# A cached decode step of two attention and MLP layers: one more part of K per batch kept on the chip, and layer 2's heads moved

## The chip, the cores and the metric

The kernel runs on one core of one Trainium2 chip. A core has a matrix engine (PE, whose weight loads are listed apart as PEld), a vector engine (DVE), a scalar engine (ACT), a general engine (POOL) and a queue engine (SP), which here issues every DMA. There are 16 DMA engines, an on-chip memory of 128 partitions (SBUF) and eight product banks of 128 x 512 float32 (PSUM), into which PE writes. The engines run side by side, each through its own list of instructions in order, and wait for one another by semaphores.

The metric is device time in microseconds (us), the median over runs.

## The reference

Eight sequences (batches) each decode one token of width 448. `_A_ref` is attention with 16 query heads over 8 cached K/V heads of 4096 x 256 (two query heads share one K/V head); `_B_ref` is a small mixer with an MLP, whose shifts move everything out of a sequence of length one, so that its first half adds nothing. The same caches and weights are used twice, in layer 1 and in layer 2:

```python
q = (x @ wq).reshape(B, Sq, Hq, Dh) ...
scores = jnp.einsum("bhqd,bhkd->bhqk", q, k) * (Dh ** -0.5)
p = _softmax(scores, axis=-1)
o = jnp.einsum("bhqk,bhkd->bhqd", p, v)
...
x = x + _A_ref(_layernorm(x, axis=-1), A_k_cache, A_v_cache, A_wq, A_wo)
x = x + _B_ref(_layernorm(x, axis=-1), B_w1, B_w2, B_w3, B_w4)
x = x + _A_ref(_layernorm(x, axis=-1), A_k_cache, A_v_cache, A_wq, A_wo)
x = x + _B_ref(_layernorm(x, axis=-1), B_w1, B_w2, B_w3, B_w4)
```

K and V are 134 MB each in bfloat16, and each is needed in both layers.

## The kernel before, in words

**Units and parts.** A unit is one K/V head of one batch in one layer, written (layer, batch, head): 128 units, and a few gaps (`None`). A unit has four *parts* of K and four of V, each 128 x 2048 bfloat16, 512 KB. A part of K arrives raw in a slot, is transposed by DVE into a second slot (`transposes`, L549, the instruction at L562), and is multiplied by PE with the expanded queries (`k_part`, L642). Then come the maximum (`max_reduce`, `max_mms`), the exponentials on ACT (`exps`), their turning into columns and their sums (`to_rows`, `sums`), and a few steps later the products with V (`v_part`, L620), whose results are scaled by ACT (`head_out`, L593).

**Slots.** The slab has 31 slots of one part each. K of six heads of a batch (`KEEP = 6`) stays after layer 1 for layer 2; two of these 24 parts are kept in four product banks (`park`: written by DVE at L567, brought back to a slot by ACT at L520), 22 in slots, so nine slots are left for what streams. The heads 0 and 1 (`loose`) are loaded again in layer 2. The other four banks are two for scores (`scb`, used by turns), one for the dense work (`dnb`) and one for head outputs and projections (`pyb`).

**Loads.** The list `loads` is written in advance in the order in which the parts are needed. `pump` (L510) is called wherever the program frees a slot; it issues loads while more than `RESERVE` slots are free, two parts in one DMA of 1 MB where two neighbouring slots are free and the stage allows it. With at least `ENOUGH` = 7 parts under way it rather waits for a neighbour than loads one part, in the stages marked `firm`. SP carries the issues out in order, each waiting for its slot's last reader.

**Order of the units.** `units` is written out by hand. For each batch b: layer 1's heads; then, while the *dense chain* of b runs (output projection, MLP, layer 2's queries: `mid_steps`, L261, one step of which is done at the end of each quarter of a unit), a gap, one or two *lone* units whose inputs are ready, and a gap; then (`fence`) layer 2 of batch b, then layer 1 of batch b + 1. In batches 0 to 3 two lone units stand beside the chain (16 quarters of a unit, the chain's larger products in two bursts, `spread`); in 4 to 7 one (12 quarters). For two units the products with V are put off into the chain (`ahead`, `late_v`): in batch b > 0 the loose heads 0 and 1 of layer 2 of batch b - 1; their probabilities wait in `pt_far`, of which there are `AHEAD` = 2. `plan` gives the step of every other `v_part`, six quarters after its K.

**Sharing of banks.** Head outputs go into `pyb` in turn, four columns each, 112 places, zeroed by a `memset` once (L625). The expanded queries of the next unit are built in columns 448 and up of a score bank (`expand`, L154). The dense work takes four turns of 64 columns in `dnb` (`room`, L203).

Of the kernel before, what the change touches and what calls it, by code (L numbers as in the profile page):

```python
# [21 lines left out]
AHEAD = 2  # L22
# [9 lines left out]
def kernel(  # L32
# [63 lines left out]
    qT2 = consts.tile([128, HJ, 2], BF16, name="qT2")  # L96
# [6 lines left out]
    park = [[ps1.tile([128, 512], FP32, name=f"park{i}{q}") for q in range(2)] for i in range(PARKED)]  # L103
# [50 lines left out]
    def expand(blk, qT, n, bank):  # L154

        rp = bank[:, 448 : 448 + 16 * n].rearrange("p (g d e h) -> p g d e h", d=4, e=2, h=2)
# [17 lines left out]
    n_po = (512 - PO) // 4  # L174
    OT = consts.tile([128, HJ, 2], BF16, name="OT")
# [27 lines left out]
    def room(n):  # L203

        turn[0] = (turn[0] + 1) % 4
        return dnb[:, 64 * turn[0] : 64 * turn[0] + n]
# [54 lines left out]
    def mid_steps(b, spread):  # L261
# [15 lines left out]
        hT = work.tile([128, HC], BF16, tag="hT", bufs=1)  # L277
# [7 lines left out]
        def gelu():  # L285
# [16 lines left out]
                    out=hT[:], in0=hu, scalar=1.0, in1=hx, op0=ALU.add, op1=ALU.mult  # L302
# [32 lines left out]
        q2 = qT2[:, :, b % 2].rearrange("p (i m) -> p i m", i=2)  # L335
# [33 lines left out]
    parked = {(second[-1], 4 - PARKED + i): i for i in range(PARKED)}  # L369
    GAP = None  # L370
    ahead = {b: [(2, b - 1, g) for g in loose] for b in range(1, Bn)}
    ahead[0], ahead[6] = [(1, 1, g) for g in loose], [(2, 5, 0), (1, 7, 0)]
    lone = {b: [(1, b + 2, g) for g in loose] for b in range(4)}
    lone.update({4: [(1, 6, 0)], 5: [(1, 6, 1)], 6: [(1, 7, 1)], 7: [(2, 5, 1)]})
# [4 lines left out]
    half = 4  # L379
    for b in range(Bn):  # L380
        if b:
            units += [(1, b, g) for g in heads[len(loose) :]]
        else:
            units += [(1, b, g) for g in heads[:5]] + ahead[0] + [(1, b, g) for g in heads[5:]]
        ends[len(units) - 1] = b
        at = 4 * len(units)
        ps = [(units.index(u), s) for u in ahead[b] for s in range(4)]
        late_v.update(zip(ps, [at + i for i in (4, 4, 5, 5, 6, 7, 8, 9)]))
        units += [GAP] + lone[b] + [GAP]
        fence[len(units)] = b  # L390
        units += [(2, b, g) for g in second[:half]] + ahead.get(b + 1, []) + [(2, b, g) for g in second[half:]]
    units += [(2, Bn - 1, g) for g in loose]
# [4 lines left out]

    def fresh(u, s):

        return u is not GAP and (u[0] == 1 or u[2] in loose)  # L400
# [61 lines left out]
    for i in range(4 * n_units + 8):  # L462
# [9 lines left out]
        t, q = divmod(i + 2, 4)  # L472
# [73 lines left out]

    todo = list(reversed(parts))

    def transposes(i):  # L549


        while len(parts) - len(todo) < by[i]:
# [395 lines left out]
```

## Time and profile before

| | |
|---|---|
| median of 3 runs | 1114.37 us (1114.31 to 1114.5) |
| the profiled execution | 1115.99 us |
| its span, first to last instruction | 1114.2 us |
| busy: PE, PEld, DVE, ACT, POOL | 687.9, 640.8, 550.7, 306.0, 104.1 us |
| bytes read from memory | 446.77 MB, 401 GB/s over the span |
| issues of loads of K and V | 605: 227 of 1 MB, 378 of 512 KB |
| from issue to landing, median | 13.1 us (V) and 14.0 us (K) for 1 MB; 8.1 and 8.8 us for 512 KB |

A line of the page's fifth part, or of an answer on groups, reads: line of the kernel, engine, operation, output <- input, shape, count | busy time, mean ns of one | idle time of the engine just before them and what ended it. A line of the waits reads: who waited <- for whom: us in total, times, longest. A line of a table by stretches reads: from:to in us, length, busy us of PE, PEld, DVE, ACT and POOL with the number of instructions, the granted clock of PE as a share, the share of the DMA engines' time, and the GB/s moved. In the page's rows of slices the span is cut into 40 equal ones and a digit is tenths.

### The profile page before, as it was taken

The numbers are of one execution on the slowest core, as the hardware profiler recorded it, in microseconds if no ns is written. First come the engines' busy times: TensorE is split into PE (matmuls) and PEld (weight loads), VectorE is DVE, ScalarE is ACT, GpSimd is POOL, SyncE is SP. The second block draws the span as 40 slices with busy tenths as digits, with TensorE's granted clock in tenths as the row PEclk, the third lists the DMA queues.
The fourth block names the chain that finished last, engine by engine and source line by source line (L and its number), as shares of the span: only waits on it lengthen the run. The fifth ranks groups of instructions, "written<-read, shape, count | busy, mean of one in ns | idle before, by whom it ended". The sixth has DMA issues, their size and how long they took to land.

```text
span 1114.2 us, 46349 instructions
## 1 busy us (share of the span) xinstructions
PE 687.9 (62%) x20737; PEld 640.8 (58%) x20737; DVE 550.7 (49%) x1305; ACT 306.0 (27%) x1360; POOL 104.1 (9%) x156
## 2 busy tenths in 40 slices
PE   3345675666756576565756667565756667665766
PEld 2334565565646565565655556565656566555765
DVE  4347554654446445554455535563446535554322
ACT  1112124321233212422243212422143212422242
POOL 0001001110011100110011000110011000100011
DMA  9999999999999999999999999999999999999993
GB/s 367 394 418 425 408 417 422 424 417 395 417 423 424 400 403 419 423 424 391 414 420 424 402 410 404 420 424 415 383 421 424 409 412 404 422 423 400 371 405 128
DMA packets 94503, 449.77 MB, mean 404 GB/s; under 512 B 9936, under 2 KB 15968, under 8 KB 64864
## 3 DMA queue, kind: packets, MB, share of 16 engines
q1 hardware_dynamic: 94304, 446.81, 98.4%
q8 instruction: 162, 2.65, 0.9%
q14 instruction: 37, 0.30, 0.1%
HBM read 446.77 MB, written 0.01 MB: 401 GB/s over the span
## 4 chain that ended last, share of the span: by engine, by line
DMA 39%; PE 15%; issue 6%; ACT 6%; DVE 5%; POOL 0%; SPq 0%; DVEq 0%; ACTq 0%; POOLq 0%
DMA slab<-in_A_v_cache_dram 31%; DMA slab<-in_A_k_cache_dram 9%; PE bank L630 5%; PE bank L653 4%; DVE slab L562 3%; ACT pt L720 2%; PE bank L137 1%; ACT slab L520 1%; ACT pe L689 1%; DVE small L686 1%; PE bank L676 1%; PE bank L712 1%; ACT pt_far L720 1%; PE bank L702 1%; PE bank L313 1%
## 5 line engine op out<-in xcount | busy, mean ns | idle before, releaser
L562 DVE STREAM_TRANSPOSE slab<-slab 128x512 f32<-128x512 f32 x640 | 414.6, 687 | 214.7 <-DMA slab<-in_A_k_cache_dram 167.2
L630 PEld LDWEIGHTS <-slab 128*128 128x128 bf16 x8192 | 273.1, 106 | 286.5 <-DMA slab<-in_A_v_cache_dram 223.0
L630 PE MATMUL bank<-pt,slab 128*128 128x2 bf16 x7168 | 260.5, 166 | 232.7 <-DMA slab<-in_A_v_cache_dram 161.5
L653 PE MATMUL bank<-Qblk,slab 128*128 128x8 bf16 x8192 | 297.2, 168 | 77.4 <-DVE slab L562 39.1
L653 PEld LDWEIGHTS <-slab 128*128 128x128 bf16 x8192 | 267.8, 105 | 88.2 <-DVE slab L562 46.6
L689 ACT ACTIVATE pe<-bank,small 128x32 bf16<-128x32 f32 x256 | 61.3, 295 | 406.7 <-DVE small L686 406.7
L731 POOL TENSOR_TENSOR small<-small 128x2 f32<-128x2 f32 x112 | 78.2, 698 | 773.2 <-DVE small L727 773.2
L720 ACT CAST pt<-bank 32x64 bf16<-32x64 f32 x448 | 90.8, 203 | 106.4 <-PE bank L712 102.5
L686 DVE TENSOR_REDUCE small<-bank 128x2 f32<-128x256 f32 x128 | 54.1, 423 | 103.2 <-PE bank L676 102.9
L727 DVE TENSOR_REDUCE small<-bank 128x2 f32<-128x64 f32 x128 | 27.1, 212 | 118.5 <-ACT pt L720 102.9
L166 ACT CAST Qblk<-bank 32x32 bf16<-32x32 f32 (+1 forms) x272 | 48.2, 177 | 110.7 <-PE bank L160 108.2
L676 PE MATMUL bank<-rows,small 128*128 128x128 bf16 x256 | 48.5, 293 | 11.5 <-DVE small L668 11.5
L668 DVE TENSOR_REDUCE small<-bank 128x2 bf16<-128x64 f32 x128 | 26.4, 206 | 58.5 <-PE bank L653 58.3
L630 PE MATMUL bank<-pt_far,slab 128*128 128x2 bf16 x1024 | 37.0, 166 | 26.1 <-DMA slab<-in_A_v_cache_dram 24.4
L712 PE MATMUL bank<-pe,rows 128*128 128x64 bf16 x512 | 51.3, 241 | 1.9 <-issue 1.9
L712 PEld LDWEIGHTS <-rows 128*128 128x128 bf16 x512 | 33.8, 124 | 28.4 <-issue 28.1
L702 PE MATMUL bank<-pe,small 128*128 128x64 bf16 x128 | 27.3, 213 | 30.7 <-ACT pe L689 29.4
L182 PEld LDWEIGHTS <-wo_sb 128*128 128x128 bf16 x1152 | 35.5, 104 | 8.8 <-issue 7.7
L182 PE MATMUL bank<-OT,wo_sb 128*128 128x1 bf16 x1024 | 33.2, 165 | 5.6 <-ACT OT L599 4.5
L137 PEld LDWEIGHTS <-wq_sb 128*128 128x128 bf16 x864 | 30.6, 106 | 10.3 <-issue 5.9
L520 ACT COPY slab<-park 128x1024 bf16<-128x1024 bf16 x32 | 30.1, 1029 | 9.4 <-DVE slab L562 9.3
L599 ACT ACTIVATE OT<-bank,small 128x2 bf16<-128x2 f32 x122 | 25.4, 261 | 24.1 <-PE bank L630 22.7
(113 smaller groups left out, 386.5 us busy)
## 6 DMA issues: line engine op xcount, KB each, us to landing
slab<-in_A_v_cache_dram SPq DMA_DIRECT2D x130, 1024.0 KB, 13.1
slab<-in_A_v_cache_dram SPq DMA_DIRECT2D x252, 512.0 KB, 8.1
slab<-in_A_k_cache_dram SPq DMA_DIRECT2D x97, 1024.0 KB, 14.0
slab<-in_A_k_cache_dram SPq DMA_DIRECT2D x126, 512.0 KB, 8.8
wo_sb<-in_A_wo_dram SPq DMA_DIRECT2D x4, 896.0 KB, 11.7
wq_sb<-in_A_wq_dram SPq DMA_DIRECT2D x3, 1024.0 KB, 6.8
w_sb<-in_B_w_dram SPq DMA_DIRECT2D x1, 1568.0 KB, 12.5
w_sb<-in_B_w_dram SPq DMA_DIRECT2D x3, 448.0 KB, 16.7
```

The costliest lines, as they stand in the source:

```text
L137: nc.tensor.matmul(pv[:, i, j, :], cols(big[:, c, :], m + i * half), rows[:, c, :], start=(i == 0 and j == 0 and c == 0), stop=True, skip_ ...
L166: nc.scalar.copy(dst, src)
L182: nc.tensor.matmul(y[:, c, :], chunk(wo_sb[:, k, :], c), o[:, k, :], start=False, stop=True, skip_group_check=True,)
L562: nc.vector.transpose(dst[:, q], src[:, q])
L630: nc.tensor.matmul(pos[t][:, k, :], vv[:, c, 128 * k : 128 * k + 128], pts[t][:, 8 * s + c, :], start=(t == 0 and s == 0 and c == 0 and k ...
L653: nc.tensor.matmul(scs[t][:, 2 * s + c, :, :], ktv[:, db, c, :, x], Qblk[run_of[t][0]][:, run_of[t][1], db, x, :, :], start=(db == 0 and x ...
L676: nc.tensor.matmul(mzs[t][:, 128 * h : 128 * h + 128], pm[:, h : h + 1].to_broadcast([128, 128]), ident, start=True, stop=True,)
L686: nc.vector.tensor_reduce(nm, mx, AX.X, ALU.max, negate=True)
L689: nc.scalar.activation(pe[:].rearrange("p c b h -> p h (c b)")[:, h], scs[t].rearrange("p c b h -> p h (c b)")[:, h], ACT.Exp, bias=nm[:, ...
L712: nc.tensor.matmul(pp[:, c], sel, pe[:], start=True, stop=True)
L720: nc.scalar.copy(pts[t][sl].rearrange("p (k c) h -> p k c h", c=4), pp[sl, :, :, pb, :].rearrange("p c k h -> p k c h"),)
L731: nc.gpsimd.tensor_tensor(out=rz_of[t], in0=zs, in1=mone, op=ALU.pow)
```

## The change

1. **One more part kept.** Part 3 of head 1 of every batch but batch 2 (`stays`) is kept as well, in the spare columns of the four shared banks: three of four column groups of each half in columns 128 to 511 of `dnb` and `pyb`, the fourth in columns 384 to 511 of the score banks. It is a transposed copy by DVE in four pieces. The first is written at once; the others after the maximum of a unit that uses the score bank in question (`at_max`, `put_rest`), and the raw slot is freed after the last. ACT brings them back in four pieces, after head outputs (`at_out`) and after exponentials (`at_exp`), three units ahead of use (`far` = 12). So 25 parts a batch are kept instead of 24, and one load less is in the list for seven batches.
2. **Room for it.** Head outputs have 16 places instead of 112, and half of them is zeroed at a time, fifteen times in all; `room` gives turns of 32 columns; `expand` uses columns 64 and up; `hT` lies over `hu`; layer 1's scaled outputs go into `qT1` instead of `OT`; `qT2` has one buffer.
3. **Order.** Layer 2 of batch b (2, 3, 6, 7, 0, 1, 4, 5) is followed by layer 1 of batch b + 1, as before, but only one lone unit stands beside each chain from batch 1 on, so the chain has 12 quarters there; the lone unit is head 0 of layer 1 of a batch ahead, or, in batches 5 and 7, head 0 of layer 2 of the batch before. Head 1 of layer 1 is an ordinary unit. The products with V that are put off into the chain are those of heads 6, 7, 4 and 5 of layer 2 of batch b - 1: four units instead of two, two parts a quarter.

```diff
-AHEAD = 2
+AHEAD = 4
...
-    park = [[ps1.tile([128, 512], FP32, name=f"park{i}{q}") for q in range(2)] for i in range(PARKED)]
+    park = []
+    for i in range(PARKED):
+        park.append([(q, 0, 4, ps1.tile([128, 512], FP32, name=f"park{i}{q}")[:]) for q in range(2)])
+    spare = [(q, 0, 3, x[:, 128:512]) for q, x in enumerate((dnb, pyb))]
+    park.append(spare + [(q, 3, 4, scb[q][:, 384:512]) for q in range(2)])
...
-        rp = bank[:, 448 : 448 + 16 * n].rearrange("p (g d e h) -> p g d e h", d=4, e=2, h=2)
+        rp = bank[:, 64 : 64 + 16 * n].rearrange("p (g d e h) -> p g d e h", d=4, e=2, h=2)
...
-    n_po = (512 - PO) // 4
+    n_po = (128 - PO) // 4
...
-        return dnb[:, 64 * turn[0] : 64 * turn[0] + n]
+        return dnb[:, 32 * turn[0] : 32 * turn[0] + n]
...
+    parked[(1, 3)] = PARKED
...
-    ahead = {b: [(2, b - 1, g) for g in loose] for b in range(1, Bn)}
-    ahead[0], ahead[6] = [(1, 1, g) for g in loose], [(2, 5, 0), (1, 7, 0)]
-    lone = {b: [(1, b + 2, g) for g in loose] for b in range(4)}
-    lone.update({4: [(1, 6, 0)], 5: [(1, 6, 1)], 6: [(1, 7, 1)], 7: [(2, 5, 1)]})
+    lone = {0: [(1, 2, 0), (1, 2, 1)], 1: [(1, 3, 0)], 2: [(1, 4, 0)], 3: [(1, 5, 0)], 4: [(1, 6, 0)], 5: [(2, 4, 0)], 6: [(1, 7, 0)], 7: [(2, 6, 0)]}
+    mix = [(2, 2), (2, 3), (2, 6), (2, 7), (2, 0), (2, 1), (2, 4), (2, 5), (1, 0), (1, 1), (1, 2), (1, 3), (1, 4), (1, 5), (1, 6), (1, 7)]
+    held_heads = [6, 7, 4, 5]
...
+        hs = [(2, b - 1, g) for g in held_heads] if b else [(1, 1, 0)]
+        ps = [(units.index(u), s) for u in hs for s in range(4)]
+        late_v.update(zip(ps, [at + i for i in (4, 4, 5, 5, 6, 6, 7, 7, 8, 8, 9, 9, 10, 10, 11, 11)]))
...
+    def stays(b, g, s):
+
+        return g not in loose or (g == 1 and s == 3 and b != 2)
...
+        for far in (2, 12):
+            t, q = divmod(i + far, 4)
+            if t < n_units and units[t] and units[t][0] == 2 and stays(*units[t][1:], q) and (units[t][2], q) in parked:
+                if (units[t][2] in loose) == (far > 2):
+                    loads.append(("p", t, q))
...
+    at_out, at_exp, at_max = [], ([], []), ([], [])
+
+    def bring(x, pieces, now):
+
+        dst = slots[x].rearrange("p (e q c x) -> p q c e x", e=4, q=2, c=4)
+
+        def move(q, lo, hi, home):
+            src = home.bitcast(BF16).rearrange("p (c e x) -> p c e x", c=4, e=hi - lo)
+            nc.scalar.copy(dst[:, q, :, lo:hi], src)
+
+        for n, p in enumerate(pieces):
+            if now:
+                move(*p)
+            else:
+                (at_out if n < 2 else at_exp[n - 2]).append(lambda p=p: move(*p))
...
+    def put_rest(t):
+
+        if at_max[t % 2]:
+            raw, rest, n = at_max[t % 2].pop(0)
+            if rest[0]:
+                rest[0]()
+                rest[0] = None
+            rest[1 + n]()
+            if not any(r for r, _, _ in at_max[1 - n] if r == raw):
+                let_go(raw)
...
+                if g in loose:
+                    put(*pieces[0])
+                    rest = [lambda p=p: put(*p) for p in pieces[1:]]
+                    for n in range(2):
+                        at_max[n].append((raw, rest, n))
+                    continue
...
-            if nth[t] == n_po // 2:
-                nc.vector.memset(pyb[:, PO : PO + 4 * (len(order) - n_po)], 0.0)
+            if n > n_po // 2 and n % (n_po // 2) == n_po // 4:
+                at = PO + 2 * n_po * (1 - n // (n_po // 2) % 2)
+                nc.vector.memset(pyb[:, at : at + 2 * n_po], 0.0)
...
+        if at_exp[t % 2]:
+            at_exp[t % 2].pop(0)()
...
                     k_part(t, q)
+                    if q == 3 and at_max[t % 2]:
+                        max_reduce(t)
+                        put_rest(t)
+                        maxed.add(t)
```

## The prediction

> **What bounds the kernel now.** I read the page from the top: busy shares, slices, DMA queues, chain.
>
> ```profile
> PE 687.9 (62%) x20737; PEld 640.8 (58%) x20737; DVE 550.7 (49%) x1305; ACT 306.0 (27%) x1360; POOL 104.1 (9%) x156
> ...
> DMA  9999999999999999999999999999999999999993
> GB/s 367 394 418 425 408 417 422 424 417 395 417 423 424 400 403 419 423 424 391 414 420 424 402 410 404 420 424 415 383 421 424 409 412 404 422 423 400 371 405 128
> ...
> q1 hardware_dynamic: 94304, 446.81, 98.4%
> ...
> DMA 39%; PE 15%; issue 6%; ACT 6%; DVE 5%; POOL 0%; SPq 0%; DVEq 0%; ACTq 0%; POOLq 0%
> ```
>
> No compute engine is above 62%, while the 16 DMA engines are busy in every slice but the last. The busy digit hides something: in slices marked 9 the rate moves between 367 and 425 GB/s. So the kernel is bound by how many bytes are loaded and by how well the queue is kept full. The waits say the same: matmuls that multiply V, and transposes of K, wait for landings.
>
> ```profile
> PE bank L630 <- DMA slab<-in_A_v_cache_dram: 186.0, 158, 4.2
> DVE slab L562 <- DMA slab<-in_A_k_cache_dram: 167.2, 77, 8.9
> ...
> PE bank L630 <- ACT qT L599: 34.6, 18, 6.6
> ...
> PE bank L630 <- ACT OT L599: 11.2, 14, 1.0
> ```
>
> Then I cut the span at the stages: the dense chain of a batch (from its first gap to the fence), layer 2 of that batch, layer 1 of the next. Columns: stretch, length, busy times, granted clock, DMA share, GB/s.
>
> ```profile
> 338.00:382.60 44.60, 28.91 (x918) 27.27 (x916) 23.88 (x51) 11.66 (x56) 4.18 (x6) 1.00 1.01 421
> 382.60:419.60 37.00, 25.57 (x767) 24.04 (x765) 14.90 (x49) 8.31 (x40) 3.34 (x5) 1.00 1.01 394
> 419.60:470.80 51.20, 29.12 (x871) 26.95 (x869) 29.03 (x59) 17.49 (x71) 4.88 (x7) 1.00 1.02 421
> ...
> 648.40:678.00 29.60, 20.29 (x600) 19.31 (x601) 10.99 (x40) 6.53 (x32) 2.64 (x4) 1.00 1.02 414
> ...
> 771.30:802.00 30.70, 20.11 (x604) 19.32 (x604) 12.55 (x42) 6.54 (x32) 2.64 (x4) 1.00 1.00 390
> 802.00:849.10 47.10, 29.32 (x902) 27.84 (x900) 24.79 (x54) 18.09 (x75) 4.88 (x7) 1.00 1.02 417
> ...
> 1016.50:1046.80 30.30, 20.11 (x602) 19.09 (x603) 10.84 (x39) 6.54 (x32) 2.63 (x4) 1.00 1.01 399
> 1046.80:1062.60 15.80, 11.20 (x355) 10.68 (x353) 4.49 (x11) 6.22 (x22) 1.40 (x2) 1.00 0.95 342
> 1062.60:1095.80 33.20, 22.55 (x722) 21.54 (x720) 9.12 (x22) 11.33 (x50) 2.91 (x5) 1.00 0.98 407
> 1095.80:1114.20 18.40, 10.38 (x299) 9.60 (x296) 5.35 (x25) 2.60 (x12) 4.58 (x5) 1.00 0.01 3
> ```
>
> A calm stage runs at 421 GB/s; I call that full rate and price every slower stage by length x (1 - rate/421). Dense chains of batches 1 to 7 run at 400, 394, 396, 414, 390, 412 and 399 and lose 1.9, 2.4, 2.2, 0.5, 2.3, 0.6 and 1.6 us: 11.4 us. Layer 2 loses nothing in batches 1 to 3, 2.1 us in 4 to 6 together and 4.1 us in 7 (rows 342 and 407). Layer 1 loses 3.8 us, most of it (405 GB/s, 1.8 us) ahead of batch 4's chain. The last 18.4 us load nothing.
>
> **The change, part by part.**
>
> *Bytes.* The list of loads falls from 320 to 313 parts of K; V stays at 512. A part is 512 KB, 0.524 MB, 1.245 us at 421 GB/s: 7 x 1.245 = 8.7 us less. DMA issues go from 605 to 604; the pairs of parts (1 MB) among them from 227 to 221. Stretches of single parts stream at 414 at best, 0.02 us more a part, and 5 more parts come singly: 0.1 us, left out. This is the one term on the path throughout: with the queue full, a part less is 1.245 us less.
>
> *The work that replaces those loads.* DVE loses 14 transposes at 687 ns (9.6 us) and gains 28 into the product banks with the same columns in all; by L567 (684 ns for 512 columns) also 9.6 us. ACT gains 28 copies: 1,029 ns for 1,024 columns (L520), two such per part, 7 x 2.06 = 14.4 us. Five more expansions of q (68 to 73) add about 0.25 us of PE and 0.7 us of ACT each. POOL's work is unchanged. DVE is half idle and ACT nearly three quarters; behind them PE waits 186 us for V. Cost taken: nothing; the cover is PE's wait for landings, 23 us a batch, and if it were gone ACT's 14.4 us would be the price.
>
> *Holds on the product banks.* The trace shows a V matmul waiting for ACT's read of another head's columns of the same bank (34.6 and 11.2 us), so two engines take turns at a bank. In the changed order some 15 more V matmuls wait for DVE: the piece of K written into that bank (three quarters of 684 ns, behind a maximum of 206 ns: 0.7 us), and the zeroing of the head sums, now fifteen times instead of once (112 ns; PE waited 1.7 us for the one there is).
>
> ```profile
> L625 DVE MEMSET bank<- x1: 112/112/112, 513.7 to 513.7; 128x64 f32 x1
> ...
>   PE bank L630: 1.7, 1
> ```
>
> ACT's copies back add 0.8 us (V bank) and twice 0.26 us (score banks); the two small pieces 0.2 us each. Per batch 0.7 + 0.8 + 0.5 + 0.4 = 2.4, times 7 = 17, and 14 x 1.7 = 24 of zeroing: 41 us of holds. Behind a held PE queue the V slots, their release and so SP's next issue. It costs time only if all loads issued have landed before PE goes on; 7 to 18 parts are issued ahead, 9 us or more. Bounds 0 and 41 us; I take 1, near the lower end, since PE waits 186 us for landings.
>
> *Dense chains.* From batch 1 on each now has 30 parts to consume in 12 steps (29 in two); before it was 30 in 16 steps (batches 0 to 3) and 22 in 12 (4 to 7). Batch 0's has 26 in 16 and is left as it was. In the short chains the queue thins at the end, where PE waits through the dense steps with no V to free slots: by finer stretches the part after the first gap runs at 412, 386, 413 and 390 GB/s, 0.4, 1.8, 0.4 and 1.4 us lost; the first gap 417, 399, 410 and 417, mean 0.2. In the long ones the first gap is worse (365 in batch 3, 1.1 us), with twice as many K parts, each of which needs two slots. The new chain has the short one's four K parts and the long one's load. I take 0.2 for the gap and 0.8 for the rest, between the 0.5 that 28 us at 414 lose and the short chains' mean of 1.0: 7 x 1.0 = 7.0, 4.4 us better than 11.4. Bounds: 0.7 each (6.5 better); batch 2's 2.4 plus 0.1 for the longer stretch (6.1 worse).
>
> *Layer 2.* With V of heads 6, 7, 4 and 5 put off, V is consumed in twos of heads with two units without between. Counting issues and releases in the order of the program, mostly 7 to 9 parts are under way from the end of the third unit to the sixth, where before there were mostly 8 to 12 in batches 1 to 3. I take 0.6 us a batch, between 0 (those batches) and 0.9 (batch 6 before): 3.6 against 2.1 for six batches, 1.5 worse; bounds 2.1 better, 3.2 worse.
>
> *Layer 1.* The three losses before lie where 7 parts are under way with five slots free, waiting for a neighbour to make a pair. In the new order this occurs in three batches again; 2.8 against 3.8, 1.0 better. Bounds 3.8 better, 0.
>
> *The end.* Batch 7's layer 2 loses 4.1 us: SP issues nothing from 1050.5 to 1056.8 us. Now its chain takes eight more V parts and 11 or 12 instead of 9 or 10 are under way there. I take half back, 2.0; bounds 0 and 3.0. The dense tail of 18.4 us is untouched.
>
> Sum: 8.7 - 1.0 + 4.4 - 1.5 + 1.0 + 2.0 = 13.6 us. The profiled execution took 1115.99 us around a span of 1114.2; it would be 1102.4. The median of the runs, 1114.37, is 1.6 lower: **1100.8 us**.
>
> **Rivals.**
>
> *Only the bytes.* Chains, layer 2 and end lose what they lose now: 1114.4 - 8.7 = 1105.7. For it: the start of a chain is slow in every batch, whatever its length. Against: the losses at its end and in batch 7 have a cause that the new order removes.
>
> *Layer 2 thins.* If its stages run at 407 GB/s, as 1062 to 1096 did, 49 us lose 1.6 in six batches, 9.8 instead of 2.1: 1105.7 + 7.7 = 1113.4, no measurable change. For it: the smaller number under way. Against: before, with 8 or 9 under way for a unit in batch 3, the stage still ran at 421.
>
> *The holds show: slower.* PE, held at the product banks, frees V slots late and the queue runs dry each time. All of the 41 us with the bytes alone: 1105.7 + 41 = 1146.7; it decides once 8.7 us, a fifth of the holds or 1.2 us a batch, reach the queue. For it: 45.8 us of such waits are in the trace already. Against: stages with those waits run at 421.
>
> The Trainium skill has a rule on this ("PSUM — Partial Sum Buffer", section on bank collisions): no two engines may be at one bank and quadrant of partitions at once, so software guards by bank, not by address. By that rule every piece of K in these banks is a hold as counted; were the guard by address the holds, and this rival, would vanish and the sum be 1.0 us better. The trace's 34.6 us agree with the guard by bank.
>
> **How the numbers follow.** Chances: the forecast 0.52, only the bytes 0.20, layer 2 thins 0.14, holds 0.14. Off the forecast's terms the chain alone could cost 10.5 us (from 4.4 better to 6.1 worse), layer 2 another 1.7, the end 2.0: taken as independent, 11 us upward, 1112. Downward 2.1, 3.6, 2.8, 1.0 and 1.0: 5.2, 1095.5. This range leaves out the holds and the upper part of the thin layer 2. A change below 0.2% (2.2 us) can't be told from none here: faster takes the first two cases and two thirds of the third, 0.81; same 0.05; slower 0.14.
>
> **What would show it.** DMA bytes on the queue down by 3.67 MB; dense chains near 38 us at 405 GB/s or more, without the thin stretch before the fence; layer 2 at 415 or more; the stretch after the last fence well above 342. Wrong if chains stay at 395 (only the bytes), if layer 2 falls to about 407, or if waits of the V matmul for DVE and ACT grow by tens of us while the slices show rates below those of before at the same places.

## The result, and the profile after

The changed kernel takes 1110.66 us (median of five, 1108.65 to 1112.04) against 1114.43 for the kernel before on the same chip: a ratio of 0.9961, interval 0.9950 to 0.9972. By the medians that is 3.8 us less, by the ratio, which the rest of the text goes by, 4.3; 13.6 were forecast. The profiled execution took 1112.03 us around a span of 1110.2.

The page of the changed kernel: busy shares, busy tenths and rates of the 40 slices, the load queue, and the engines' shares of the chain that ended last.

```profile
PE 689.6 (62%) x20757; PEld 646.7 (58%) x20757; DVE 552.1 (50%) x1333; ACT 322.3 (29%) x1408; POOL 104.4 (9%) x156
...
DMA  9999999999999999999999999999999999999992
GB/s 360 396 416 423 409 405 419 425 397 416 419 417 405 416 417 425 423 408 397 419 367 424 408 416 409 415 413 407 416 424 425 408 399 390 415 389 414 408 418 92
...
q1 hardware_dynamic: 94160, 443.14, 98.2%
...
DMA 52%; PE 19%; ACT 10%; DVE 10%; issue 7%; SPq 2%; POOL 0%; DVEq 0%; ACTq 0%
```

The bytes fell by the 3.67 MB of seven parts (446.81 to 443.14 MB), yet the rate over the span fell from 401 to 399 GB/s. There are fewer slices at 383 to 395, but a new hole: 367 GB/s in the 21st slice, inside layer 2 of batch 3. In the chain that ended last ACT and DVE stand at 10% each, before at 6 and 5; but the chain of before could be followed back to 318 us only, and its shares add up to 71%. From 318 us on, ACT and DVE are 8 and 7% of it before, 12 and 9% after.

The waits of the changed kernel (who waited <- for whom: us in total, times, longest):

```profile
PE bank L688 <- DMA slab<-in_A_v_cache_dram: 152.9, 154, 3.2
DVE slab L605 <- DMA slab<-in_A_k_cache_dram: 148.6, 55, 10.0
...
PE bank L688 <- DVE bank L683: 19.9, 15, 2.6
PE bank L688 <- ACT qT L650: 15.5, 25, 1.0
...
PE bank L734 <- DVE bank L611: 6.7, 5, 1.9
PE bank L688 <- DVE bank L611: 5.9, 3, 4.3
PE bank L688 <- ACT slab L531: 3.7, 3, 1.2
PE bank L762 <- ACT slab L531: 3.2, 6, 0.9
PE bank L141 <- ACT slab L531: 2.4, 2, 1.2
```

The new holds at the shared banks are there at the size counted. The third line is the zeroing; the last five are the pieces, first DVE's, then ACT's copies back. They are 41.8 us in all, where I counted 41 (19.9 for the 24 of zeroing, 21.9 for the 17 of pieces). The old holds for ACT's read of head outputs fell, from 45.8 to 15.5 us, which I had not counted and which no run explains. With the 1.7 us of the one zeroing before, all holds of this kind rose by 10 us only, from 47.5 to 57.3.

The same cut by stretches (from:to, length, busy us of PE, PEld, DVE, ACT, POOL, granted clock, DMA share, GB/s): chain of batch 2, layer 2, layer 1; chain of batch 3, layer 2, layer 1; layer 2 of batch 6; then the chain of batch 7, its layer 2 in two stretches, and the tail.

```profile
361.70:398.10 36.40, 24.65 (x731) 23.09 (x730) 9.07 (x38) 7.40 (x36) 2.65 (x4) 1.00 1.03 417
398.10:444.40 46.30, 28.85 (x869) 26.87 (x867) 30.81 (x65) 17.61 (x71) 4.90 (x7) 1.00 1.02 422
444.40:493.40 49.00, 31.18 (x963) 28.93 (x960) 29.45 (x62) 13.25 (x64) 4.90 (x7) 1.00 1.01 420
493.40:530.90 37.50, 24.33 (x729) 23.01 (x729) 8.90 (x37) 7.39 (x36) 2.65 (x4) 1.00 1.01 396
530.90:579.60 48.70, 28.59 (x868) 26.79 (x866) 30.71 (x64) 19.26 (x75) 4.90 (x7) 1.00 0.98 390
579.60:627.00 47.40, 30.95 (x964) 29.23 (x963) 28.15 (x59) 13.25 (x64) 4.90 (x7) 1.00 1.01 417
...
920.60:958.90 38.30, 24.60 (x735) 23.06 (x733) 24.73 (x54) 16.94 (x66) 4.20 (x6) 1.00 1.00 393
...
1005.40:1042.00 36.60, 23.16 (x731) 22.49 (x729) 8.89 (x37) 7.40 (x36) 2.64 (x4) 1.00 1.03 410
1042.00:1057.80 15.80, 11.07 (x358) 10.67 (x356) 5.70 (x13) 4.35 (x20) 1.41 (x2) 1.00 1.03 417
1057.80:1090.60 32.80, 21.67 (x689) 20.68 (x687) 9.08 (x23) 15.17 (x56) 3.39 (x5) 1.00 0.94 390
1090.60:1110.20 19.60, 11.22 (x326) 10.44 (x325) 5.35 (x25) 2.61 (x12) 4.11 (x5) 1.00 0.01 3
```

The clock is 1.00 throughout. The chains now run at 396 to 417 over some 37 us, and the stretch behind the last fence rose from 342 to 417, as forecast. Layer 2 does not hold its rate: 390 GB/s in batch 3 and 393 in batch 6, where only batch 7 had lost much before. The tail without loads grew from 18.4 to 19.6 us.

I priced every stretch of a trace as the prediction did, by the bytes of the load queue alone (419 GB/s where the whole moves 421). The us lost, in one profiled execution each, also for five experiments told of below:

| | chains 1 to 7 | layer 2, batches 0 to 6 | layer 2, batch 7 | layer 1 | tail |
|---|---|---|---|---|---|
| before | 11.9 | 3.2 | 4.2 | 3.6 | 18.4 |
| changed | 8.0 | 9.7 | 2.6 | 5.4 | 19.6 |
| no third part | 9.2 | 3.1 | 2.6 | 5.2 | 17.4 |
| third part for nothing | 9.0 | 5.1 | 2.2 | 2.7 | 19.1 |
| less waiting for pairs | 12.2 | 8.5 | 2.2 | 2.5 | 19.0 |
| two heads held (mended) | 13.0 | 8.3 | 5.1 | 0.8 | 19.5 |
| two, in batch 7 four | 13.2 | 9.3 | 2.2 | 2.0 | 19.8 |

From the first row to the second: bytes 8.7 less (3.67 MB at 419 GB/s), chains 3.9 less, the end 1.6 less; layer 2 of the other batches 6.5 more, layer 1 1.8 more, the tail 1.2 more, chain 0 and the first 75 us 0.4 more each. Sum 3.9 less, where the spans differ by 4.0. (Each figure is of one execution, and up to half a us hangs on where the stretches are cut; the same stretch moves by a us between kernels that load in the same order.)

### The profile page after: what moved, and what is told of

The parts are those of the page before. It is cut to its first block, busy times and chain, and to the rows that moved or that the text cites. A ratio compares the mean times of both kernels' runs of the same rounds, so it can differ in the third digit from the quotient of the medians.

```text
span 1110.2 us, 46432 instructions
## 1 busy us (share of the span) xinstructions
PE 689.6 (62%) x20757; PEld 646.7 (58%) x20757; DVE 552.1 (50%) x1333; ACT 322.3 (29%) x1408; POOL 104.4 (9%) x156
## 3 DMA queue, kind: packets, MB, share of 16 engines
q1 hardware_dynamic: 94160, 443.14, 98.2%
## 4 chain that ended last, share of the span: by engine, by line
DMA 52%; PE 19%; ACT 10%; DVE 10%; issue 7%; SPq 2%; POOL 0%; DVEq 0%; ACTq 0%
DMA slab<-in_A_v_cache_dram 39%; DMA slab<-in_A_k_cache_dram 12%; PE bank L688 7%; DVE slab L605 6%; PE bank L711 5%; ACT pt L780 3%; ACT slab L531 2%; ACT pe L747 2%; DVE small L744 2%; PE bank L734 2%; PE bank L772 1%; PE bank L141 1%; SPq L562 1%; ACT pt_far L780 1%; PE bank L762 1%
## 5 line engine op out<-in xcount | busy, mean ns | idle before, releaser
L605 DVE STREAM_TRANSPOSE slab<-slab 128x512 f32<-128x512 f32 x626 | 405.1, 686 | 182.7 <-DMA slab<-in_A_k_cache_dram 148.6
L688 PE MATMUL bank<-pt,slab 128*128 128x2 bf16 x6336 | 230.4, 166 | 187.5 <-DMA slab<-in_A_v_cache_dram 117.1
L791 POOL TENSOR_TENSOR small<-small 128x2 f32<-128x2 f32 x99 | 69.3, 700 | 707.2 <-DVE small L787 707.2
L780 ACT CAST pt<-bank 32x64 bf16<-32x64 f32 x396 | 80.5, 203 | 79.2 <-PE bank L772 75.7
L688 PE MATMUL bank<-pt_far,slab 128*128 128x2 bf16 x1856 | 65.1, 166 | 43.0 <-DMA slab<-in_A_v_cache_dram 35.8
L170 ACT CAST Qblk<-bank 32x32 bf16<-32x32 f32 (+1 forms) x292 | 51.4, 176 | 102.1 <-PE bank L164 99.4
L772 PEld LDWEIGHTS <-rows 128*128 128x128 bf16 x512 | 33.7, 124 | 47.5 <-issue 47.1
L650 ACT ACTIVATE qT<-bank,small 128x2 bf16<-128x2 f32 x198 | 41.8, 266 | 46.8 <-PE bank L688 37.0
L185 PE MATMUL bank<-qT,wo_sb 128*128 128x1 bf16 (+1 forms) x1152 | 38.8, 165 | 8.3 <-ACT qT L650 5.4
L650 ACT ACTIVATE qT<-bank,rz_far 128x2 bf16<-128x2 f32 x58 | 12.2, 265 | 84.6 <-PE bank L688 84.5
L734 PEld LDWEIGHTS <-small 128*128 128x128 bf16 x256 | 17.4, 106 | 31.6 <-DVE small L726 28.4
```

The source lines that it names most:

```text
L170: nc.scalar.copy(dst, src)
L185: nc.tensor.matmul(y[:, c, :], chunk(wo_sb[:, k, :], c), o[:, k, :], start=False, stop=True, skip_group_check=True,)
L605: nc.vector.transpose(dst[:, q], src[:, q])
L650: nc.scalar.mul(qT1[:, k : k + 2, b], pos[t][:, :, h], rz_of[t][:, h : h + 1])
L688: nc.tensor.matmul(pos[t][:, k, :], vv[:, c, 128 * k : 128 * k + 128], pts[t][:, 8 * s + c, :], start=(n_v[0] == 1 and s == 0 and c == 0 a ...
L734: nc.tensor.matmul(mzs[t][:, 128 * h : 128 * h + 128], pm[:, h : h + 1].to_broadcast([128, 128]), ident, start=True, stop=True,)
```

## The experiments

Each kernel was timed against the kernel before on the same chip. The median of before lies between 1114.4 and 1116.7 us on these chips, so I compare ratios; one per mille is 1.1 us. Differences of two ratios are uncertain by about 1.7 per mille, 1.9 us. The ratio of the changed kernel was measured on one chip; that it holds on the chips of the experiments is assumed.

At first there were three theories. **Q**: the load queue runs thin because the planner leaves slots free while it waits for a neighbour, and because the third part takes slots. **H**: PE waits at the shared product banks, and this reaches the queue. **O**: the new order by itself thins layer 2.

**Less waiting for pairs.** `ENOUGH = 7` becomes `ENOUGH = 10`.

> The changed kernel, with ENOUGH raised from 7 to 10: a load of one part waits for a neighbouring slot only while 10 parts or more are under way (660 issues instead of 604, the same bytes). Three theories on why 8.7 us of loads less gave 4: (Q) the queue of loads is thin in layers 1 and 2, because the planner leaves five to nine free slots empty, waiting for a neighbour with seven parts under way, and the third kept part takes slots; (H) the waits at the shared product banks, some 42 us in the trace after, reach the end; (O) the new order of the heads by itself thins layer 2. Q expects 1105 to 1108 us against 1110.7, and the stretches of 264 to 385 GB/s in layer 2 of batch 3 and layer 1 ahead of batches 1, 2 and 7 gone. H and O expect 1110 to 1112, or more for the single parts.

Measured: 0.9961 (0.9943 to 0.9980), the ratio of the changed kernel, so not what Q expects of the planner. Layer 1 loses 2.9 us less and the chains 4.2 more (table). With this order the planner's waiting decides where the queue is thin, not how much is lost.

**Each zeroing 16 times over.**

```diff
-                nc.vector.memset(pyb[:, at : at + 2 * n_po], 0.0)
+                for _ in range(16):
+                    nc.vector.memset(pyb[:, at : at + 2 * n_po], 0.0)
```

> The changed kernel, with each of the 15 zeroings of the head sums done 16 times over: 15 x 85 ns = 1.3 us more each, so the 19.9 us that V matmuls wait for them become some 39. Q and O expect no change that matters, 1109 to 1113 us, since PE then waits that much less for landings. H expects 5 to 19 us more, 1116 to 1130.

Measured: 1.0135 (1.0115 to 1.0154), 19.4 us above the changed kernel by the ratios, 19.6 by the medians. Its waits:

```profile
DVE slab L605 <- DMA slab<-in_A_k_cache_dram: 136.7, 48, 9.1
...
PE bank L689 <- DMA slab<-in_A_v_cache_dram: 121.2, 122, 4.0
...
PE bank L689 <- DVE bank L684: 57.7, 15, 4.7
```

So holds of the V bank do reach the end once they are long enough: 37.8 us more of them (57.7 against 19.9) go with 19.4 us more time. PE's wait for V did shrink, from 152.9 to 121.2 us, as a cover should, and the time rose all the same. SP's waits show the way: a load is issued when its slot's last reader is done, and SP waited 31.7 us longer for V matmuls to be done with slots (first in the changed kernel, then here):

```profile
SPq L562 <- PE bank L688: 258.9, 230, 6.9
```

```profile
SPq L562 <- PE bank L689: 290.6, 217, 6.9
```

But DVE itself was also taken up longer. It is busy 19.1 us more (571.2 against 552.1), and its memsets of 85 ns follow one another with 82 ns between, so that a row of sixteen lasts 2.6 us (from the timeline: start, length), some 37 us more in all. Hence the next one.

```profile
160.17 2.58 DVE L684 MEMSET bank<- 128x32 f32 x16
```

**The same DVE time at no bank.** 23 memsets of two columns in SBUF behind each zeroing.

> The changed kernel with 23 more memsets of two columns in SBUF behind each of the 15 zeroings, about 20 us of DVE time in all, as much as the kernel with each zeroing done 16 times (1130.2 us) but at no product bank. If the 19.6 us there were holds of the bank: 1110 to 1112. If they were DVE's time (K's transposes late): 1128 to 1131.

Measured: 1.0006 (0.9997 to 1.0015), 5.0 us above the changed kernel: neither of the two. The group of the added memsets, in its answer on groups:

```profile
L685 DVE MEMSET small<- 128x2 f32 x345 | 20.7, 60 | 25.7 <-POOL small L793 4.2
```

A row of 23 lasts some 2.8 us here (60 ns each, 67 between), so DVE was taken up for 42 us, a little longer than by the rows of sixteen. The V matmuls wait no longer than in the changed kernel: 19.1 us for 15, going on 0.05 to 0.15 us after the zeroing. So 42 us of DVE's time, 20.7 of them busy, that PE's bank never sees cost 5.0 us, an eighth. The rest of the 19.4, some 14 us, is the hold of the bank. The first half of this was a surprise: DVE is idle half of the time.

**No third part.** `stays` returns `g not in loose`; the seven parts are loaded again.

> The changed kernel without the third kept part: order, banks and zeroing as changed, but part 3 of head 1 is loaded again in layer 2 (8.7 us of loads more, 7 raw slots not held, 7 slots not taken three units ahead, 28 pieces less each way). If the part is worth its bytes (O, or H for the zeroing alone): 1118 to 1120 us. If it pays back part of them in a thinner queue (Q) or in bank waits of its pieces (H): 1112 to 1116, with layer 1 and 2 nearer 419 GB/s.

Measured: 0.9995 (0.9984 to 1.0006). The new order with its zeroing is worth 0.5 us, no more than none, and the third part 3.4 per mille, 3.8 us, of its 8.7, as Q and H expect. Layer 2 loses 3.1 us here (table), no more than before, which speaks against O.

**No third part, and head outputs over 112 places with one zeroing, as before.** On top of the last: `n_po = (512 - PO) // 4`, one `memset`.

> The same without the third part, and with 112 places for head sums and one zeroing as before the change (the 19.9 us of waits for zeroing go). H expects 3 us or more faster than the run without the third part alone; Q and O expect the same time within 1.5 us.

Measured: 0.9986 (0.9976 to 0.9996). The 14 further zeroings cost 0.9 per mille, 1.0 us, if anything, though PE waits 15.0 us for them in the run above. At this size the zeroing's holds are no answer.

**The third part for nothing.** It is neither loaded nor kept: layer 2 multiplies its neighbour in its stead, so the scores of seven parts are those of other columns.

```diff
+        if p == 2 and g in loose and stays(b, g, s):
+            key = u, 2
```

> The changed kernel with the same 313 parts of K loaded, but the third part of a batch is neither put into the product banks nor copied back: layer 2 multiplies the part next to it in its stead (so seven parts of its scores are those of other columns), and the part's slot of layer 1 is let go at once. The kernel without the third part took 1114.0 us, the changed one 1110.7, seven parts at full rate are 8.7 us. If keeping the part costs something (its slots, or its pieces at the shared banks), this gives the rest of the 8.7 us back: 1105 to 1106.5. If bytes not loaded are worth less than full rate in this order, because the queue is thin just there (a part without its neighbour is loaded singly), it stays at 1110 to 1111.

Measured: 0.9922 (0.9910 to 0.9935). Against no third part that is 7.3 per mille, 8.1 us for seven parts: bytes not loaded are worth about their full rate. (The 14 transposes of these parts are left out with them, 9.3 us of DVE in the traces of the two runs, so the 8.1 are not of the bytes alone.) Against the changed kernel it is 3.9 per mille: *keeping* the third part costs 4.3 us.

**The third part written and brought back at once**, so that its slots are held a shorter time: no list `at_max`, `far` 4 instead of 12, four copies in one go.

> The changed kernel, with all four pieces written in one go, so that the raw slot is let go at once (before, after the last piece, up to two units later), and brought back by four copies in one go one unit ahead instead of piece by piece three units ahead. The same pieces, the same banks, the same bytes; a slot held for some 5 and some 8 steps less per batch. If slots are what keeping costs: 1106 to 1108.5, and the stretch after the fence of batch 3 (373 GB/s in the changed kernel) streams at 410 or more. If the waits at the shared banks are what it costs, no gain or a small loss: 1110 to 1113, since DVE and ACT now hold the score banks in longer runs.

Measured: 0.9976 (0.9967 to 0.9985), 1.7 us slower than the changed kernel, if anything. Slots let go sooner don't help; but PE's waits for the pieces are longer here (36.3 us against 21.9), so this run alone doesn't part slots from holds. The next one does.

**The slots of the third part, without its work.** Every step stays in its place, but DVE writes no piece and ACT copies none back (layer 2 multiplies what lies in the slot).

```diff
-                    nc.vector.transpose(dst, src[:, q, :, lo:hi])
+                    if g not in loose:
+                        nc.vector.transpose(dst, src[:, q, :, lo:hi])
...
-            nc.scalar.copy(dst[:, q, :, lo:hi], src)
+            if now:
+                nc.scalar.copy(dst[:, q, :, lo:hi], src)
```

> The changed kernel with every step of the third part in the order of the program (the raw slot held until where its last piece would be written, a slot taken three units ahead of layer 2's head, the maximum taken early) but without its work: no piece is written into the product banks by DVE and none copied back by ACT, so layer 2 multiplies what lies in the slot. The same loads in the same order, the same number of parts under way as the changed kernel at each step. Against the kernel in which the third part costs nothing (7.8 per mille under before) the changed kernel (3.9 per mille under before) loses 4.3 us. If the slots cost them: about 4 per mille under before. If the pieces at the shared banks do: about 7.5 per mille under before. In between: the share of each.

Measured: 0.9922 (0.9910 to 0.9935), the ratio of the kernel in which the part is for nothing. So the slots cost nothing that can be measured, and the theory that I liked best by then fell: Q's second half. The reading that had led me to it was the thin stretch in layer 2 of batch 3. Of the two kernels, one has it and the other not (layer 2's later part, first without the slots, then with them):

```profile
546.00:577.70 31.70, 17.89 (x533) 16.71 (x531) 18.46 (x39) 13.44 (x52) 3.49 (x5) 1.00 1.01 424
```

```profile
546.80:577.60 30.80, 17.75 (x532) 16.62 (x530) 18.58 (x39) 13.53 (x52) 3.49 (x5) 1.00 0.99 391
```

The rate differs by 8%, the length not: the first kernel moved more bytes there and was thin elsewhere. A stage that streams slowly is not by itself lost time.

**Only ACT's copies left out.** The second half of that diff alone.

> The same with DVE's 28 pieces written into the banks, and only ACT's 28 copies back left out (layer 2 multiplies what lies in the slot). Against the one before, it gives the share of DVE's pieces; against the changed kernel, that of ACT's copies (14.4 us of ACT, put at nothing in the forecast). By the priced holds, DVE's pieces (0.7 + 0.4 of 2.4 us a batch) and ACT's copies (1.3 of 2.4) would each be half of what the pieces cost in all.

Measured: 0.9942 (0.9929 to 0.9956). DVE's pieces cost 2.0 per mille, 2.2 us, ACT's copies 1.9 per mille, 2.1 us: about half each, together the 4.3, but each uncertain by 1.9.

**The pieces at other banks.** The same instructions, but the third part lies in the four banks of the two parts parked before, where PE multiplies nothing (the part parked there later overwrites it, so layer 2 multiplies other columns).

```diff
-    spare = [(q, 0, 3, x[:, 128:512]) for q, x in enumerate((dnb, pyb))]
-    park.append(spare + [(q, 3, 4, scb[q][:, 384:512]) for q in range(2)])
+    spare = [(q, 0, 3, park[0][q][3][:, 0:384]) for q in range(2)]
+    park.append(spare + [(q, 3, 4, park[1][q][3][:, 0:128]) for q in range(2)])
```

> The changed kernel, but DVE writes the 28 pieces of the third part into the four banks that hold the two parts parked before, and ACT copies them back from there: the same instructions with the same columns and the same steps, at no bank that PE multiplies into (what the pieces hold is lost to the head parked there later, so layer 2 multiplies other columns at the third part). Against the kernel without pieces (7.8 per mille under before) the pieces cost 3.9 per mille, 4.3 us. If that is the hold of the shared banks: 7.5 to 8 per mille under before. If it is the time of DVE and ACT: 3.5 to 4.5 per mille under before.

Measured: 0.9951 (0.9939 to 0.9964). 1.0 per mille better than the changed kernel, 2.9 worse than without the pieces: 4.9 per mille under before, between the two cases expected. So some 3 of the 4.3 us stay when no bank of PE is touched, which speaks for the work of DVE and ACT rather than the hold. It is not settled: the two shares are not cleanly apart (1.1 and 3.2 us, each uncertain by 1.9), and this kernel has a wait of its own, 6.2 us:

```profile
DVE park L611 <- ACT slab L531: 6.2, 3, 3.4
```

**Two heads held instead of four.** `held_heads = [4, 5]`.

> The changed kernel with V of two heads (4 and 5) instead of four put off into the dense chains from batch 1 on; V of heads 6 and 7 is consumed right behind its scores. 8 parts fewer for each of seven chains (22 for 12 steps). If putting off four heads is what thins layer 2 (7.7 us lost behind the third unit, against 1.2 before): that falls to 4 or less, the chains lose 2 to 4 more, and the time is 1107 to 1111. If the four heads earn what I forecast (4.4 us in the chains, 2.0 at the end) and layer 2 is thin for another reason: 1113 to 1117.

Measured: 1.0027 (1.0016 to 1.0038). This run is spoilt at its end. In `put_rest`, `any(r for r, _, _ in ...)` takes slot number 0 for none, so with batch 7's third part in slot 0 that slot was released twice, and could be given out while in use. In the changed kernel the third part never lies in slot 0. Mended to `any(r == raw ...)`:

> The kernel with V of two heads held, but with every slot released once. In the run before it, slot 0 was released twice in batch 7's stretch: a comparison in the third part's release treats slot number 0 as none, which the changed kernel never meets, and then two loads went to one slot one after the other. If its loss at the end (7.9 us in the last 37 us of loads) was of that, it goes back to the changed kernel's 2 to 3 and the time is 5 us lower: 1112 to 1114. If the two heads themselves thin the end: 1116 to 1118 again.

Measured: 1.0002 (0.9992 to 1.0013), between the two cases expected: the double release had cost 2.8 us. Four heads are worth 4.1 per mille, 4.6 us, over two. Where that comes from shows in the stretches: chain of batch 3 with the three units behind it and the rest of layer 2 in the changed kernel (its layer 1 stands above, from 579.60 on); then the same two and layer 1 in the mended run, and its batch 7 behind the fence:

```profile
493.40:547.20 53.80, 35.18 (x1065) 33.11 (x1065) 19.42 (x58) 12.32 (x57) 4.05 (x6) 1.00 1.01 402
547.20:579.60 32.40, 17.74 (x532) 16.70 (x530) 20.19 (x43) 14.33 (x54) 3.49 (x5) 1.00 0.95 377
```

```profile
503.90:548.50 44.60, 30.82 (x937) 29.24 (x936) 19.54 (x57) 11.46 (x53) 4.04 (x6) 1.00 1.01 393
548.50:586.90 38.40, 21.22 (x661) 19.87 (x658) 19.98 (x43) 14.95 (x58) 3.49 (x5) 1.00 1.01 424
586.90:635.00 48.10, 30.80 (x959) 29.02 (x959) 28.38 (x61) 13.21 (x64) 4.88 (x7) 1.00 1.01 423
1043.20:1059.30 16.10, 10.91 (x356) 10.54 (x354) 4.39 (x11) 6.24 (x22) 1.40 (x2) 1.00 1.01 397
1059.30:1091.80 32.50, 22.01 (x697) 21.02 (x695) 8.85 (x22) 12.86 (x53) 2.79 (x4) 1.00 0.90 368
```

With two heads held, layer 2's later part and layer 1 are at full rate (424 and 423) in nearly every batch, and the chains starve (393, with the units behind them). With four the chains are fuller (402) and layer 2 and layer 1 thin (377 and 417). The loss moves with the V that is moved.

**Two heads, and four in batch 7 alone** (slots released once).

> V of two heads (4 and 5) held in batches 1 to 6 and of four in batch 7, slots released once. In batches 0 to 6 the run with two heads lost 0.5 us in layer 2's later part and layer 1 and about 17 in chains and the units behind them; three heads 8 and 13. By those sums two and three are within 4 us of each other; if the end (2 us with four, 7.9 with two) is what made two heads slow, this is 1107 to 1111.

Measured: 0.9976 (0.9967 to 0.9985), 1112.6 us, just above the range expected if the end is what counts. Of the 4.6 us, 2.9 come from batch 7 and 1.7 from the six batches ahead of it, each uncertain by some 1.6.

**Three heads held: 7, 4 and 5; 3, 4 and 5; 6, 4 and 5** in batches 1 to 6, four in batch 7. The list, for the first:

```diff
-        hs = [(2, b - 1, g) for g in held_heads] if b else [(1, 1, 0)]
+        hs = [(2, b - 1, g) for g in (held_heads if b == Bn - 1 else [7, 4, 5])] if b else [(1, 1, 0)]
```

> The changed kernel with V of three heads (7, 4 and 5) put off into the chains of batches 1 to 6, and of four into that of batch 7; V of head 6 is consumed right behind its scores. With two held, layer 2's later part and layer 1 lost 0.5 us between them in batches 0 to 6 and the chains with the units behind them 17 (with four: 11 and 10). If losses go straight with the number held, three is worth what four is, 1110 to 1112, and only the end is safe. If layer 2 is thin because two heads in a row, 6 and 7, free no V slots, while the chains only need enough V to fill twelve steps, three takes most of both: 1105 to 1108.5, with layer 2's later part at 415 or more in the batches 1 to 6.

> The same with heads 3, 4 and 5 put off, so that V of heads 6 and 7 is consumed ahead of the two heads that load K. In the order of the program 8 or 9 parts more often are under way here at heads 3 and 6, and 11 to 13 at heads 7, 0 and 1. If it is the number held alone that counts: the same as with 7, 4 and 5, within 1.5 us. If it counts where the gap without V lies: up to 3 us slower, with the loss in the first units of layer 2.

> The kernel with V of heads 3, 4 and 5 held, with every slot released once. In the run before it slot 0 was released twice in batch 5 and PE then waited 10 us three times for a load just issued. If that was all of its loss: within 1.5 us of the kernel with heads 7, 4 and 5 (6.2 per mille under before). If the place of the gap counts: up to 3 us above that one.

> The same with heads 6, 4 and 5 held instead of 7, 4 and 5, and the old limit. With 7, 4 and 5 the ratio is 0.9938, with 3, 4 and 5 0.996, with four heads 0.9961. If it is the number held that sets the trade between chains and layer 2: between 0.9935 and 0.9965, not to be told from the other threes.

Measured: 0.9938 (0.9924 to 0.9952) with 7, 4, 5; 0.9960 (0.9945 to 0.9974) with 3, 4, 5; 0.9975 (0.9964 to 0.9986) with 6, 4, 5. The first run of 3, 4, 5 stood at 1.0121 (1.0105 to 1.0136): there slot 0 was released twice from batch 5 on, and PE waited 10 us at a time for a load only just issued; mended, the 18 us are gone. (With 7, 4, 5 the third part never lies in slot 0.) The list 6, 4, 5 came out above the 0.9965 expected for it. The three lists lie around the changed kernel's 0.9961, 2.6 us below to 1.6 above, and the number of parts under way in the order of the program, by which I chose them, did not foretell which.

**Three heads (7, 4, 5) with `ENOUGH = 10`.**

> V of heads 7, 4 and 5 held in batches 1 to 6 and of four in batch 7, and the planner waits for a neighbour only with 10 parts under way instead of 7: no step is left with eight or fewer under way and four slots free (37 before), at the price of 672 issues for 600. Three heads with the old limit stood at 6.2 per mille under before. If the losses left in layer 1 and in layer 2 are of waiting for pairs: 8 per mille under before or better. If, as with four heads, single loads lose elsewhere what waiting lost: 5.5 to 7.

Measured: 0.9972 (0.9956 to 0.9989), 3.8 us slower than with the old limit and outside both ranges expected. With four heads the same limit changed nothing. Either waiting for pairs is worth something with three heads, or the 0.9938 was a lucky measurement; no run here parts the two.

The lowest ratio of a kernel that computes all of it is thus 0.9938, 2.6 us under the changed one, and the two intervals just touch. It is the best of five lists of one kind, so I don't call it a version that beats the change.

## Why the prediction was right or wrong

The forecast was 1100.8 us. The time, 1110.66, lies inside the range (1095.5 to 1112.0) and on the side given 0.81, but the gain is a third of the one forecast. That it lies inside is luck: the range got its width upward from the chains, which came out nearly as said, while the work that replaces the loads had no width in it at all. (In the chances, two thirds of the rival "Layer 2 thins" were put under faster, though it was priced at 1113.4, no measurable change.) By the terms of the sum:

**Bytes: 8.7 forecast, 8.1 measured** (no third part against third part for nothing, with 14 transposes gone as well). Right within the uncertainty of 1.9.

**The work that replaces those loads: 0 forecast, about 3 to 4 measured.** This is the step that failed first: "Cost taken: nothing; the cover is PE's wait for landings". The work was a little more than counted: ACT's copies 16.5 us (14.4 counted) and DVE's pieces 12.2 us (9.6), from the answer on groups by shape:

```profile
L531 ACT COPY slab<-bank 128x768 bf16<-128x768 bf16 x14 | 11.2, 799 | 0.0
L611 DVE STREAM_TRANSPOSE bank<-slab 128x384 f32<-128x384 f32 x14 | 7.9, 563 | 0.0
L531 ACT COPY slab<-bank 128x256 bf16<-128x256 bf16 x14 | 5.3, 375 | 0.0
L611 DVE STREAM_TRANSPOSE bank<-slab 128x128 f32<-128x128 f32 x14 | 4.3, 305 | 0.2
```

But that is not what failed. 28.7 us of such work cost 4.3 us, with what holds are in it, and 42 us of DVE taken up by memsets that nothing needs cost 5.0. PE's wait for landings is no cover: PE waits because the queue is thin, and a slot that DVE or ACT let go later makes it thinner. The traces show that link in SP's waits, summed over all loads of K and V. It waited for engines to be done with slots 621 us in the changed kernel, 640 with the added memsets and 660 with the zeroing 16 times over, and for landings 178, 164 and 156 us. For the pieces themselves the link is not shown: the kernel with the slots alone has 609 us, but the one with the part for nothing, just as fast, has 619 (one execution each).

**Holds: 1.0 forecast, 1 to 2 measured** (of which the pieces' part is in the 4.3 above). 41 us counted, 41.8 in the trace; the zeroing costs 1.0 us when it is undone, and the pieces gain 1.1 at other banks, both within their uncertainty of none. The rival that the holds show has a mechanism that exists, but sets in later than it said: at "8.7 us, a fifth of the holds" it would have decided, and of the 41.8 us here 1 to 2 reached the end, while 37.8 us more cost some 14. The Trainium skill ("PSUM — Partial Sum Buffer", section on bank collisions) has software guard these banks by bank and quadrant of partitions, not by address. The trace agrees with a guard by bank, since V matmuls waited 19.9 us for the zeroing of columns that none of them wrote at that time.

**The order: 5.9 forecast, about 1.5 measured** (0.9995 without the third part is 0.5 us, and 1.0 of zeroing is to be added, which the forecast has under holds). Its terms, from the table, changed kernel against before:

- Dense chains: 4.4 forecast, 3.9 in the trace. Their length (36 to 40 us) and the end of the thin stretch ahead of the fence came as said; two of the seven ran below the 405 GB/s named (396 and 401). Single parts streamed at up to 417 GB/s (chain of batch 2), not at "414 at best".
- The end: 2.0 forecast; 1.6 in the queue, of which the tail gives 1.2 back. "The dense tail of 18.4 us is untouched" was wrong by that, in this execution; without the third part it was 17.4.
- Layer 2: 1.5 worse forecast, 6.5 worse in the trace of batches 0 to 6, above its bound of 3.2. This is the term that was mis-sized most in the changed kernel. The rival "Layer 2 thins" had a loss of 9.8 us, and 9.7 came; but its cause, the order, is not what the runs show. Without the third part the same stretches lose 3.1, no more than before, and with the part for nothing 5.1. In these traces the excess thus comes with the third part, and the 4.3 us above are a part of it: the two must not be added.
- Layer 1: 1.0 better forecast, 1.8 worse in the trace. It was read off steps at which the planner waits for a neighbour; with less waiting layer 1 lost 2.9 less and the chains 4.2 more, and the time was the same.

What the sum did wrong as a whole is to treat the stages as separate accounts. With 31 slots and some 10 parts under way, V put off into the chain is V that does not free slots in layer 2. From two heads held to four, chains and end gain 7.5 us and layer 1 and the rest of layer 2 lose 6.0 by the table; in time 4.6 come out (of these two profiled executions the first was 2.1 us under its median, the second 1.4 above).

Term by term the forecast missed by 0.6 (bytes), 4.3 (what keeping the part costs) and 4.4 (the order): 9.3 us, all that is missing. They add up because each is the step from one measured kernel to the next. Open is why layer 2 thins just where it does, and how the 4.4 divide. The trace without the third part has 1.7 of them in the chains (9.2 lost where 4.4 better than 11.9 was forecast) and 2.6 in layer 1; but the profiled execution of before was 1.6 us above its median and that one 0.8 below, so single traces can't settle sizes like these.

## What to carry to other kernels

An engine that is half idle is no free place for work when the queue lives on the slots it releases: here a us of DVE and ACT time cost 0.12 to 0.15 us. Bytes not loaded were worth about their full rate here, but take what is done in their place out of that, by a run in which they are neither loaded nor replaced. And in a ring of slots a stage that streams slowly is a place where the loss shows, not the account it belongs to: move the load and it shows elsewhere.

## What the runs showed of the hardware

A zeroing of 32 columns takes 85 ns on DVE and held the V matmul 1.3 us on average (19.9 us for 15). The length of the hold is what DVE has ahead of the zeroing in its own order: in five of the fifteen two transposes of 0.7 us each, and PE went on within 0.2 us of the zeroing's end.

Sixteen in a row are 1.36 us of busy DVE, but last 2.6 us from the first to the last, 82 ns lying between two of them. They held the V matmul 3.8 us (57.7 for 15), 2.5 longer than a single one, and each such row cost 1.3 us of time (19.4 for 15). Rows of 2.8 us at no bank of PE's cost 0.33 us each (5.0 for 15). So DVE's time cost about four times as much at a product bank as elsewhere, but only in long rows: the single zeroings cost 1.0 us for all 14, if anything.
